# Top-k attention with a squared-ReLU feed-forward: the softmax sums by ScalarE's accumulator, their reciprocals by a power on GpSimd

## The chip, the cores and the metric

One core of a Trainium2 chip. The metric is the device time of one execution in microseconds; the median of the runs counts. The core's engines are named as in the profile: PE (TensorE; PEld are its weight loads), DVE (VectorE), ACT (ScalarE), POOL (GpSimd) and SP (SyncE, which here issues DMAs). Each works through its own queue in order.

## The reference

```python
B, H, S, D = q.shape                       # 8, 8, 576, 64
scores = np.matmul(q, k.transpose(0, 1, 3, 2)) / np.sqrt(D)
kth = np.partition(scores, -32, axis=-1)[..., -32:-31]
scores = np.where(scores >= kth, scores, -1e9)
scores = scores - np.max(scores, axis=-1, keepdims=True)
attn = np.exp(scores)
attn = attn / (np.sum(attn, axis=-1, keepdims=True) + 1e-09)
attn_out = np.matmul(attn, v)              # 8, 8, 576, 64
x = attn_out.transpose(0, 2, 1, 3).reshape(B * S, H * D)      # 4608 x 512
h = np.maximum(x @ w_in, 0.0)              # w_in 512 x 2048
out = (h * h @ w_out).astype(np.float32)   # w_out 2048 x 512
```

Of each row of 576 scores the 32 largest are kept, then softmax, then the product with the values; the result goes through two matrix products with a squared ReLU between.

## The kernel before

The attention is a list of 144 steps (`U = 144`). A step handles two row blocks of 128 rows (x = 0 and 1), mostly the same rows of two heads, so every tile of scores is 128 partitions x 2 x 576. The order of all instructions is written out by hand in one loop, `for u in range(U)`, and `pin` keeps each engine's queue in that order. Several steps are in work at once. In iteration u:

- GpSimd drops the entries of step u-1 that are under its 32nd largest: `drop` writes a very negative number, as bytes, into `gone` (L409, once per x), and a DMA issued by GpSimd adds that to the scores `s` (L413; in the first steps an addition on GpSimd, L411).
- VectorE runs the search for the 32 largest of step u: `quads_of` (L323, L324, which open an iteration on VectorE), then `topk` in four rounds of MAX8 (L374) and three of MATCH_REPLACE8 (L378). The last round is the pair of MAX8 over 576 columns (288 + 144 in the first 11 steps). Between rounds 2 and 3 stands `pairs_of(u+1)` (L314, L315).
- TensorE computes the scores of step u+1 (L285, two halves `sc_a`, `sc_b`); ScalarE copies them to `s` (L294). Between the two halves stands `in_gap`: the products of the weights with the values for step u-4 (`weigh`, L461), into the one accumulator `av`. The values carry a column of ones, so column 64 of the product is the sum of the weights.
- VectorE takes the reciprocal of that column (`invert`, L475), and ScalarE multiplies by it in `place` (L494, L499), both for step u-4.
- ScalarE computes the exponentials of step u-2 (`exps`, L417), and SP turns them by a transposing DMA into `wT` (`turn`, L426).
- GpSimd makes the smaller partners of pairs by integer arithmetic on the bits: `both(u+1)` (L338: sum of the two halves) and `lesser(u+1)` (L347: less the larger, which ScalarE's copy `most` (L330) gives it). The last round of MAX8 of step u+1 reads what L347 writes.
- In 40 of the steps GpSimd has one more small operation behind L347 on the results of `topk` (L384 to L386, 128 x 36).
- At the end come pieces of the feed-forward (`dense`, `piece`: L579, L586, L594, L630), two to three a step, and ScalarE's `negate` (L394: the negated largest and 32nd largest, for the exponentials and the drop).

So on GpSimd the order in an iteration is: two drops, DMA issue, `both`, `lesser`, now and then a test. On ScalarE it is: copies of scores, preparation of later heads, two placings, two exponentials, `most`, casts, `negate`, ReLU and square.

```python
if ok(u - 4):
    invert(u - 4)
...
if ok(u - 4):
    place(u - 4)
...
if ok(u - 2):
    exps(u - 2, 0)
    exps(u - 2, 1)
    turn(u - 2)
```

After the loop the products, reciprocals and placings of the last four steps follow; the last two steps use other PSUM banks and TensorE's transposes.

Of the kernel before, what the change touches and what calls it, by code (L numbers as in the profile page):

```python
# [13 lines left out]
f32 = mybir.dt.float32  # L14
# [9 lines left out]
def kernel(  # L24
# [9 lines left out]
    nc = tc.nc  # L34
# [10 lines left out]
    def pin(ins):  # L45
        tc.keep_in_program_order(ins)
        return ins
# [224 lines left out]
    def scores(u, between=None):  # L272
# [15 lines left out]
        if not between:  # L288
            half(js[1])
        s = scp.tile([128, 2, S], f32, name="s", bufs=4)  # L290
        st[u] = {"s": s, "ps": ps}
# [99 lines left out]
    def negate(u, ends):  # L391
        neg = small.tile([128, 2, 2], f32, name="neg", bufs=4)
# [22 lines left out]
    def exps(u, x):  # L415
        d = st[u]
        pin(nc.scalar.activation(w_two[u % 3][:, x, 0:S], d["s"][:, x, :], AF.Exp, bias=d["neg"][:, x, 0:1]))  # L417

# [5 lines left out]
    def turn(u):  # L424
        wT = scp.tile([128, 9, 128], bf16, name="wT", bufs=3)
        pin(nc.sync.dma_start_transpose(out=wT[:, :, :], in_=w_two[u % 3][:, :, :].rearrange("p x n -> p (x n)")))  # L426
        st[u]["wT"] = wT
# [7 lines left out]
    def turn_by_tensor(u, x):  # L435
        if "tp" not in st[u]:
            st[u]["wT"] = scp.tile([128, 9, 128], bf16, name="wT", bufs=3)
# [34 lines left out]

    def invert(u):
        r = small.tile([128, 2, 1], f32, name="rsum", bufs=4)
        pin(nc.vector.reciprocal(r[:, :, :], sums(u)[:, :, 64:65]))  # L475
        st[u]["r"] = r
# [206 lines left out]
    def most_ups(u):  # L683
        if u < U - 26:
            return 1 if downs else 2
        return 2 if u >= U - 20 or len(ups) > 4 else 1

    def in_gap(u):
        products(u - 4)
        if moves:  # L690
            moves.pop(0)()()
# [52 lines left out]
    pin(nc.gpsimd.memset(ones[:, :], 1.0))  # L744
    worst = const.tile([128, 1], f32, name="worst")
    load_weights(2)
    scores(0)
# [18 lines left out]
    def products(w):  # L766
        if ok(w):
            for x in range(2):
                weigh(w, x)
# [6 lines left out]
    for u in range(U):  # L776
# [18 lines left out]
        if u == 0:  # L795
            in_gap(u)
        if ok(u - 4):
            invert(u - 4)
        casts_next = bool(soon) and soon[0].__name__ == "values"
        for _ in range(0 if casts_next else 2 if u < 8 else 1):  # L800
            prepare(u)
        if ok(u - 4):
            place(u - 4)
        turn_x(u)
        moves.extend(soon_moves)
        soon_moves.clear()
        if u == U - 1:
            moves.pop(0)()()
            fill_scores(KH // 2)
        if ok(u - 2):  # L810
            exps(u - 2, 0)
            exps(u - 2, 1)
            turn(u - 2)
        fetch(4 if u < 12 else 3)
# [5 lines left out]
        if ok(u + 1):  # L820
            pairs_of(u + 1)
            copy_far(u + 1)
            lesser(u + 1)
            if tests:
                pin(tests.pop(0)())
        topk(u, (3,))
        if casts_next:
# [7 lines left out]
        if u < U - 1:  # L835
            dense(u, 0)
            st[u]["neg"] = negate(u, 2)
            dense(u, 1)
        else:
            piece(True)  # L840
            piece(True)
# [22 lines left out]
    one.square()  # L864
    invert(U - 4)
    place(U - 4)
# [11 lines left out]
    products(U - 3)  # L878
    invert(U - 3)
    place(U - 3)  # L880
# [152 lines left out]
```

## Time and profile before

| | |
|---|---|
| median of 3 runs | 905.09 us (904.73 to 907.03) |
| the profiled execution | 905.09 us |
| its span | 903.0 us |
| granted TensorE clock | 0.948 |
| busy: PE, DVE, ACT, POOL | 678.7, 881.8, 760.1, 779.0 us |

The profile shows one execution. A row of the timeline gives the start and the length in microseconds, the engine, the line of the kernel, the operation with what it writes and reads, how many in a row are merged (x2), and in brackets how long the engine had been idle before, with what ended that wait. A row of the groups gives the line, the operation, the count, busy time in us and mean length in ns, and then the idle time before these instructions and what ended it. Successive instructions of one engine overlap a little, so a length says less than the distance to the next start.

### The profile page before, as it was taken

How to read it: one execution, taken by the hardware profiler on the slowest of the kernel's cores; microseconds unless marked ns; L12 is line 12 of the kernel's file. 1: busy time of each engine (PE TensorE's matmuls, PEld its weight loads, DVE VectorE, ACT ScalarE, POOL GpSimd, SP SyncE). 2: the span in 40 equal slices, each digit the busy share in tenths (PEclk: the TensorE clock that was granted, in tenths of full speed). 3: DMA queues.
4: the chain of work that ended last, by engine and by line, in shares of the span. 5: the costliest groups of instructions: out<-in, count | busy, mean ns of one | idle time of the engine just before them, and what ended most of it. 6: DMA issues, size and time to landing. Idle time of an engine off the chain costs nothing.

```text
span 903.0 us, 21007 instructions
## 1 busy us (share of the span) xinstructions
PE 678.7 (75%) x6274; PEld 424.6 (47%) x6274; DVE 881.8 (98%) x3635; ACT 760.1 (84%) x1752; POOL 779.0 (86%) x818
## 2 busy tenths in 40 slices
PE   5777777777777777767687777677777777887796
PEld 3334454445444445444454444444444444554455
DVE  6999999999999999999999999999999999999995
ACT  3566799889988898888988899988999888997883
POOL 7999988988988888898898888998898988899880
PEclk9989999999999999999999999998999999999999
DMA  6699989899999999899899999999899999687762
GB/s 147 106 155 207 179 186 191 192 197 203 194 193 184 199 190 197 190 192 210 186 201 185 195 194 191 199 196 191 189 206 186 209 202 214 145 162 181 158 142 53
DMA packets 290778, 164.78 MB, mean 182 GB/s; under 512 B 258145, under 2 KB 268641, under 8 KB 290657
## 3 DMA queue, kind: packets, MB, share of 16 engines
q1 hardware_dynamic: 267408, 80.29, 48.0%
q0 software_dynamic: 21904, 82.65, 40.6%
q8 instruction: 52, 0.85, 0.4%
q14 instruction: 70, 0.57, 0.2%
q10 hardware_dynamic: 1344, 0.43, 0.2%
HBM read 37.75 MB, written 9.44 MB: 52 GB/s over the span
## 4 chain that ended last, share of the span: by engine, by line
DVE 74%; issue 12%; ACT 5%; PE 4%; DMA 2%; POOL 2%; SPq 0%; POOLq 0%; DVEq 0%; ACTq 0%
DVE m L374 31%; DVE cat L378 20%; DVE sc_b L314 6%; DVE most L315 5%; DVE cat L324 5%; DVE cat L323 5%; ACT s L294 1%; DVE rsum L475 1%; DMA s<-gone_b 1%; ACT rl L586 1%; DMA s<-gone_a 1%; POOL cat L347 1%; PE dn_ps L630 1%; PE sc_b L285 1%; ACT x_tok L494 0%
## 5 line engine op out<-in xcount | busy, mean ns | idle before, releaser
L374 DVE MAX8 m<-cat 128x8 f32<-128x104 f32 (+3 forms) x1152 | 435.4, 416 | 0.0
L378 DVE MATCH_REPLACE8 cat<-m,cat 128x104 f32<-128x104 f32 (+2 forms) x864 | 260.7, 306 | 0.0
L338 POOL TENSOR_TENSOR cat<-s 128x576 int32<-128x576 int32 (+1 forms) x144 | 238.6, 1657 | 2.7 <-ACT s L294 2.7
L347 POOL TENSOR_TENSOR cat<-cat,most 128x576 int32<-128x576 int32 (+1 forms) x144 | 196.1, 1362 | 25.0 <-DVE m L374 7.5
L285 PE MATMUL sc_b<-qkT 64*128 64x288 f32 x512 | 107.4, 494 | 88.4 <-DVE cat L324 84.2
L285 PE MATMUL sc_a<-qkT 64*128 64x288 f32 x512 | 97.3, 453 | 95.4 <-DVE most L315 39.2
L579 PEld LDWEIGHTS <-w_in 128*128 128x128 bf16 x2304 | 146.2, 101 | 38.6 <-issue 15.7
L630 PE MATMUL dn_ps<-w_out,h 128*128 128x512 bf16 x560 | 159.5, 416 | 0.3 <-ACT h L594 0.3
L579 PE MATMUL gen<-xT,w_in 128*128 128x128 bf16 x2016 | 137.1, 224 | 2.2 <-ACT xT L538 1.4
L409 POOL TENSOR_SCALAR gone_a<-s,neg 128x576 uint8<-128x576 f32 x143 | 107.1, 749 | 16.0 <-ACT neg L394 4.8
L409 POOL TENSOR_SCALAR gone_b<-s,neg 128x576 uint8<-128x576 f32 x142 | 106.3, 749 | 12.6 <-ACT neg L394 0.9
L294 ACT ACTIVATE s<-sc_b 128x576 f32<-128x576 f32 x144 | 93.4, 648 | 25.4 <-PE sc_b L285 21.5
L285 PEld LDWEIGHTS sc_a<-qkT 64*128 64x128 f32 x512 | 41.4, 186 | 123.4 <-issue 33.3
L294 ACT ACTIVATE s<-sc_a 128x576 f32<-128x576 f32 x144 | 91.3, 634 | 4.9 <-PE sc_a L285 3.2
L285 PEld LDWEIGHTS sc_b<-qkT 64*128 64x128 f32 x512 | 43.9, 198 | 103.8 <-PE av_ps L461 63.5
L394 ACT ACTIVATE neg<-m 128x4 f32<-128x4 f32 (+1 forms) x145 | 29.9, 206 | 70.6 <-DVE m L374 69.6
L594 ACT ACTIVATE h<-rl 128x512 bf16<-128x512 f32 x136 | 85.7, 630 | 4.3
L586 ACT ACTIVATE rl<-gen 128x512 f32<-128x512 f32 x142 | 83.0, 586 | 0.7 <-PE gen L579 0.6
L630 PEld LDWEIGHTS <-h 128*128 128x128 bf16 x560 | 53.3, 104 | 61.6 <-issue 26.3
L461 PEld LDWEIGHTS <-wT 128*128 128x128 bf16 (+1 forms) x1600 | 54.5, 100 | 54.4 <-issue 43.9
L413 POOL DMA_DIRECT2D s<-gone_b x67 | 59.3, 885 | 22.0 <-DVE m L374 9.0
L413 POOL DMA_DIRECT2D s<-gone_a x66 | 58.3, 884 | 20.4 <-DVE m L374 12.0
(172 smaller groups left out, 1248.6 us busy)
## 6 DMA issues: line engine op xcount, KB each, us to landing
s<-gone_b POOLq DMA_DIRECT2D x67, 576.0 KB, 4.6
s<-gone_a POOLq DMA_DIRECT2D x66, 576.0 KB, 4.8
v_raw<-in_v_dram SPq DMA_DIRECT2D x64, 128.0 KB, 3.3
k_raw<-in_k_dram SPq DMA_DIRECT2D x63, 128.0 KB, 3.4
q_raw<-in_q_dram SPq DMA_DIRECT2D x63, 128.0 KB, 3.2
out_dram<-wide SPq DMA_DIRECT2D x31, 256.0 KB, 3.0
v_raw<-in_v_dram SPq DMA_DIRECT2D x64, 32.0 KB, 3.0
w_in<-in_moe_w_in_dram POOLq DMA_DIRECT2D x8, 256.0 KB, 4.7
```

Of the source, the lines that this page charges most:

```text
L285: pin(nc.tensor.matmul(out=ps[j][:, x, 0:HALF], lhsT=lhsT, rhs=rhs, start=True, stop=True))
L294: pin(nc.scalar.activation(s[:, :, j * HALF:(j + 1) * HALF], ps[j][:, :, 0:HALF], AF.Copy))
L338: pin(tt(less, s[:, :, 0:wide].bitcast(i32), s[:, :, HALF:HALF + wide].bitcast(i32), op=ALU.add))
L347: pin(tt(less, less, d["most"][:, 0:n_h, :, :].bitcast(i32).rearrange("p h x n -> p x h n"), op=ALU.subtract))
L374: pin(nc.vector.max(out=m[r][:, x, :], in_=part(r, x)))
L378: pin(nc.vector.match_replace(out=part(r, x), in_to_replace=m[r][:, x, :], in_values=part(r, x), imm_value=NEG))
L409: pin(nc.gpsimd.tensor_scalar(byte[:, x, :, 1], s[:, x, :], scalar1=d["neg"][:, x, 1:2], scalar2=-HUGE, op0=ALU.add, op1=ALU.mult))
L413: pin(nc.gpsimd.dma_start(out=s[:, :, :].rearrange("p x n -> p (x n)"), in_=byte[:, :, :, :].rearrange("p x n two -> p (x n two)").bitcast ...
L579: pin(nc.tensor.matmul(out=hp[:, n * n_rows:(n + 1) * n_rows], lhsT=w_in[:, kh, (f0 + n) * 128:(f0 + n + 1) * 128], rhs=xt(kh), start=(kh ...
L586: pin(nc.scalar.activation(kept["rl"][:, :], hp, AF.Relu))
L594: pin(nc.scalar.activation(h2, flat, AF.Square))
L630: pin(nc.tensor.matmul(out=op[:, :], lhsT=held["h2"][:, f, c * 128:(c + 1) * 128], rhs=w_out[:, f, :], start=(f == 0), stop=(f == NF - 1)))
```

## The change

- The sum of the weights is no longer taken from the product: `exps` gives ScalarE's exponentials an accumulator output, `sums`, one column for each x, for all steps but the last two.
- The reciprocals of two steps (4 columns) are made together on GpSimd, as the sums to the power of -1; this stands behind `lesser(u+1)` and the test in every second iteration. VectorE keeps the reciprocals of the last two steps.
- The exponentials and the turning move from u-2 to u-3, the products and the placings from u-4 to u-5. From step `CATCH` = 121 on they catch up: iterations 121 and 122 hold three exponentials each, from 123 on they are at u-2 again; iteration 124 holds the products and placings of two steps, and from 125 on they are at u-4.
- Deeper buffers: `s` 5 for 4, `neg` 6 for 4, `wT` 4 for 3.

```diff
     def exps(u, x):
         d = st[u]
-        pin(nc.scalar.activation(w_two[u % 3][:, x, 0:S], d["s"][:, x, :], AF.Exp, bias=d["neg"][:, x, 0:1]))
+        if u % 2 == 0 and x == 0 and u < U - 2:
+            d["sums"] = small.tile([128, 2, 2], f32, name="sums", bufs=4)
+            st[u + 1]["sums"] = d["sums"]
+        total = d["sums"][:, u % 2, x:x + 1] if u < U - 2 else None
+        pin(nc.scalar.activation(w_two[u % 3][:, x, 0:S], d["s"][:, x, :], AF.Exp, bias=d["neg"][:, x, 0:1], accum_out=total))
...
     def invert(u):
+        if u < U - 2:
+            if u % 2 == 0:
+                both_r = small.tile([128, 2, 2, 1], f32, name="rboth", bufs=4)
+                pin(nc.gpsimd.tensor_tensor(both_r[:, :, :, 0], st[u]["sums"][:, :, :], minus[:, :, :], op=ALU.pow))
+                st[u]["r"], st[u + 1]["r"] = both_r[:, 0], both_r[:, 1]
+            return
         r = small.tile([128, 2, 1], f32, name="rsum", bufs=4)
         pin(nc.vector.reciprocal(r[:, :, :], sums(u)[:, :, 64:65]))
         st[u]["r"] = r
...
+    CATCH = 121
+
+    def to_weigh(u):
+        return u - 5 if u <= CATCH + 3 else u - 4
+
+    def to_raise(u):
+        if u < CATCH:
+            return [(u - 3, 0), (u - 3, 1)]
+        if u == CATCH:
+            return [(u - 3, 0), (u - 3, 1), (u - 2, 0)]
+        if u == CATCH + 1:
+            return [(u - 3, 1), (u - 2, 0), (u - 2, 1)]
+        return [(u - 2, 0), (u - 2, 1)]
+
     def in_gap(u):
-        products(u - 4)
+        products(to_weigh(u))
...
-        if ok(u - 4):
-            invert(u - 4)
...
-        if ok(u - 4):
-            place(u - 4)
+        if ok(to_weigh(u)):
+            place(to_weigh(u))
...
-        if ok(u - 2):
-            exps(u - 2, 0)
-            exps(u - 2, 1)
-            turn(u - 2)
+        for w, x in to_raise(u):
+            if ok(w):
+                exps(w, x)
+                if x == 1:
+                    turn(w)
...
             lesser(u + 1)
             if tests:
                 pin(tests.pop(0)())
+        for w, x in to_raise(u):
+            if ok(w) and x == 1 and w % 2:
+                invert(w - 1)
         topk(u, (3,))
...
             dense(u, 0)
             st[u]["neg"] = negate(u, 2)
             dense(u, 1)
+            if u == CATCH + 3:
+                products(u - 4)
+                place(u - 4)
```

`minus` is a constant tile of -1.0, set once. The two `invert` calls of steps `U - 4` and `U - 3` behind the loop are taken out.

More of the change, by code (lines that the diff above doesn't have):

```diff
@@ L289, in scores @@
             half(js[1])
-        s = scp.tile([128, 2, S], f32, name="s", bufs=4)
+        s = scp.tile([128, 2, S], f32, name="s", bufs=5)
         st[u] = {"s": s, "ps": ps}
@@ L391, in negate @@
     def negate(u, ends):
-        neg = small.tile([128, 2, 2], f32, name="neg", bufs=4)
+        neg = small.tile([128, 2, 2], f32, name="neg", bufs=6)
         got = st[u]["ends"] if ends == 2 else st[u]["ends"][:, :, 0:1]
@@ L424, in turn @@
     def turn(u):
-        wT = scp.tile([128, 9, 128], bf16, name="wT", bufs=3)
+        wT = scp.tile([128, 9, 128], bf16, name="wT", bufs=4)
         pin(nc.sync.dma_start_transpose(out=wT[:, :, :], in_=w_two[u % 3][:, :, :].rearrange("p x n -> p (x n)")))
@@ L436, in turn_by_tensor @@
         if "tp" not in st[u]:
-            st[u]["wT"] = scp.tile([128, 9, 128], bf16, name="wT", bufs=3)
+            st[u]["wT"] = scp.tile([128, 9, 128], bf16, name="wT", bufs=4)
             st[u]["tp"] = {}
@@ L745 @@
     worst = const.tile([128, 1], f32, name="worst")
+    minus = const.tile([128, 2, 2], f32, name="minus")
+    pin(nc.gpsimd.memset(minus[:, :, :], -1.0))
     load_weights(2)
@@ L864 @@
     one.square()
-    invert(U - 4)
     place(U - 4)
@@ L878 @@
     products(U - 3)
-    invert(U - 3)
     place(U - 3)
```

## The prediction

> **What bounds the kernel now.** I read the page's busy time and chain first, then the timeline of VectorE step by step, then GpSimd's and ScalarE's, because the change takes work from the first and gives it to the other two.
>
> ```profile
> PE 678.7 (75%) x6274; PEld 424.6 (47%) x6274; DVE 881.8 (98%) x3635; ACT 760.1 (84%) x1752; POOL 779.0 (86%) x818
> ...
> DVE 74%; issue 12%; ACT 5%; PE 4%; DMA 2%; POOL 2%; SPq 0%; POOLq 0%; DVEq 0%; ACTq 0%
> ```
>
> VectorE (DVE) is busy for 98% of the span and carries the chain. What a reciprocal is worth there can be read from the first steps, since none is issued before step 4. Timeline of VectorE, step 2 (none) and step 6 (one); columns are start, length, what:
>
> ```profile
> 23.28 0.44 DVE L323 TENSOR_TENSOR cat<-sc_b,most 128x288 f32<-128x288 f32 x1
> ...
> 29.58 0.44 DVE L323 TENSOR_TENSOR cat<-sc_b,most 128x288 f32<-128x288 f32 x1
> ...
> 48.60 0.44 DVE L323 TENSOR_TENSOR cat<-sc_b,most 128x288 f32<-128x288 f32 x1
> ...
> 50.13 0.16 DVE L475 RECIPROCAL rsum<-av_ps 128x2 f32<-128x2 f32 x1
> 50.20 0.45 DVE L374 MAX8 m<-cat 128x8 f32<-128x120 f32 x2
> ...
> 54.96 0.44 DVE L323 TENSOR_TENSOR cat<-sc_b,most 128x288 f32<-128x288 f32 x1
> ```
>
> L323 opens a step. Step 2 takes 29.58 - 23.28 = 6.30 us, step 6 takes 54.96 - 48.60 = 6.36: 0.06 more. The reciprocal shows 0.16 us, but the MAX8 behind it starts 0.07 after it, under its tail. So one costs the path about 0.065, not 0.16.
>
> From step 11 (drops by DMA, wider bit sums) the stretch to step 141 is steady:
>
> ```profile
> 75.74 0.79 POOL L347 TENSOR_TENSOR cat<-cat,most 128x288 int32<-128x288 int32 x1
> ...
> 79.56 1.41 DVE L374 MAX8 m<-cat 128x8 f32<-128x576 f32 x2
> 80.88 0.44 DVE L323 TENSOR_TENSOR cat<-sc_b,most 128x288 f32<-128x288 f32 x1
> ...
> 862.41 0.43 DVE L323 TENSOR_TENSOR cat<-sc_b,most 128x288 f32<-128x288 f32 x1
> ```
>
> That is 130 steps in 781.5 us, 6.01 each. GpSimd (POOL) serves the same step, and one step in full view shows how close it is:
>
> ```profile
> 399.29 1.41 POOL L347 TENSOR_TENSOR cat<-cat,most 128x576 int32<-128x576 int32 x1
> ...
> 403.95 1.40 DVE L374 MAX8 m<-cat 128x8 f32<-128x576 f32 x2
> 404.05 0.42 ACT L330 ACTIVATE most<-sc_b 128x288 f32<-128x288 f32 x1
> ...
> 405.07 1.40 POOL L347 TENSOR_TENSOR cat<-cat,most 128x576 int32<-128x576 int32 x1
> 405.27 0.43 DVE L323 TENSOR_TENSOR cat<-sc_b,most 128x288 f32<-128x288 f32 x1
> ...
> 406.57 1.57 POOL L409 TENSOR_SCALAR gone_a<-s,neg 128x576 uint8<-128x576 f32 x2
> ...
> 407.77 0.52 ACT L494 ACTIVATE x_tok<-av_ps,rsum 128x64 bf16<-128x64 f32 x2
> ...
> 408.17 1.46 ACT L417 ACTIVATE w_two_a<-s,neg 128x576 bf16<-128x576 f32 x2
> ...
> 409.05 1.73 POOL L338 TENSOR_TENSOR cat<-s 128x576 int32<-128x576 int32 x1
> ...
> 410.86 1.41 POOL L347 TENSOR_TENSOR cat<-cat,most 128x576 int32<-128x576 int32 x1
> ```
>
> From one L347 to the next there are 410.86 - 405.07 = 5.79 us: GpSimd's own cycle when nothing holds it up, though the page calls it 86% busy. Its lead is visible too: the L347 of 399.29 ends at 400.70, and the last MAX8 pair that reads it starts at 403.95, 3.25 later; at step 10 the same lead is 79.56 - 76.53 = 3.03.
>
> **The change, part by part.**
>
> *Reciprocals leave VectorE.* 140 of the 142 stand in the loop (steps 4 to 143), the other two in the tail. 140 x 0.065 = 9.1 us, if nothing else is late: steps of 5.94.
>
> *A power joins GpSimd*, 71 of them, 128 x 4, each behind L347 of every second step. It needs no wait of its own, because L347 already waits for the copy `most`, which ScalarE issues after the exponentials concerned. Behind it stand the next two drops, their DMA issue and both bit sums. No power is in the trace. The nearest rows are the small test operations at the same place, and the same ones in the tail:
>
> ```profile
> 464.74 1.41 POOL L347 TENSOR_TENSOR cat<-cat,most 128x576 int32<-128x576 int32 x1
> 466.10 0.31 POOL L384 TENSOR_TENSOR flags<-m 128x36 f32<-128x36 f32 x1
> 466.50 1.57 POOL L409 TENSOR_SCALAR gone_a<-s,neg 128x576 uint8<-128x576 f32 x2
> ...
> 470.77 1.42 POOL L347 TENSOR_TENSOR cat<-cat,most 128x576 int32<-128x576 int32 x1
> 472.14 0.27 POOL L385 TENSOR_TENSOR flags<-m 128x36 f32<-128x36 f32 x1
> 472.49 1.57 POOL L409 TENSOR_SCALAR gone_b<-s,neg 128x576 uint8<-128x576 f32 x2
> ...
> 879.83 2.38 POOL L384 TENSOR_TENSOR flags<-m 128x36 f32<-128x36 f32 x3 [2.17 <-DVE m L374]
> ```
>
> Without a test, L347 to the drop is 406.57 - 405.07 = 1.50; with L384 it is 1.76, with L385 1.72. So a plain small operation adds 0.26 or 0.22 to the cycle. L347 spends 1.41 on 576 elements, 0.0024 each, so four elements instead of 36 save 0.08: the low end is about 0.17. In the tail three L384 in a row take 0.79 each, or 0.65 net of the 0.14 by which a small operation overlaps its neighbours: the high end among small operations. A power is several arithmetic steps on each element, so it should lie above the plain ones; I take 0.45, the middle of 0.26 and 0.65. Nothing in the trace excludes more.
>
> The Trainium skill ("Perfetto Trace Analysis", GPSIMD Engine Instruction) says to time this engine by the spacing of starts, not by reported spans; the trace bears that out, since L384's 0.31 adds 0.26. By the span the low end would be 0.23 (0.31 less the same 0.08), and the sum below 4 us higher.
>
> GpSimd's reserve in those 130 steps follows from its cycle and these groups (busy, mean ns; idle before):
>
> ```profile
> L413 POOL DMA_DIRECT2D s<-gone_b x67 | 59.3, 885 | 22.0 <-DVE m L374 9.0 <-DVE cat L378 8.5 <-POOL gone_b L409 4.5
> L413 POOL DMA_DIRECT2D s<-gone_a x66 | 58.3, 884 | 20.4 <-DVE m L374 12.0 <-DVE cat L378 7.9 <-POOL gone_a L409 0.6
> L384 POOL TENSOR_TENSOR flags<-m 128x36 f32<-128x36 f32 x24 | 9.0, 379 | 2.2 <-DVE m L374 2.2
> L385 POOL TENSOR_TENSOR flags<-m 128x36 f32<-128x36 f32 x8 | 2.1, 266 | 0.0
> L386 POOL TENSOR_SCALAR flags<-flags 128x36 f32<-128x36 f32 x8 | 2.1, 263 | 0.1
> ```
>
> Seven of the eight groups of tests fall there: 21 x 0.26 + 14 x 0.22 = 8.5. The DMA issues idle 42.4 in all, 2.5 more than 133 x 0.30. So GpSimd needs 130 x 5.79 + 8.5 + 2.5 = 763.7 of 781.5 us: a reserve of 17.8. 67 powers there at 0.45 want 30.2, 12.4 too many. GpSimd then sets the step, at about 5.87 + 0.22 = 6.10, and the MAX8 pair waits for L347.
>
> *The lead cushions little.* The new chain behind L347 is power, two placings, two exponentials, `most`, and only then VectorE's next L323: 0.45 + 0.52 + 1.46 + 0.42, and 0.25 for the sums, is 3.1, while VectorE needs 405.27 - 403.95 = 1.32 from the MAX8 pair to L323. So a lead under 1.8 holds VectorE up through ScalarE, and 3.0 - 1.8 = 1.2 can be used. Four powers and seven shorter steps before step 11 take 4 x 0.45 + 0.45 = 2.25 of lead: 1.05 too many. They also save VectorE 7 x 0.065 = 0.45.
>
> The sum: 12.4 + 1.05 - 0.45 = 13.0 us. In general it is 71 x p - 19.0 for a power of p us, zero at 0.27, and not under -9.1 plus what the end costs.
>
> *Sums by ScalarE.* Two stretches of the middle and of the end (length; busy time of PE, PEld, DVE, ACT, POOL), and the placings:
>
> ```profile
> 261.21:381.27 120.06, 89.92 (x830) 56.69 (x831) 120.06 (x501) 105.98 (x245) 105.57 (x106) 0.93 0.93 190
> ...
> 760.04:820.41 60.37, 49.69 (x498) 32.70 (x499) 60.22 (x251) 56.35 (x127) 53.23 (x56) 0.97 0.78 162
> ...
> L494 ACT ACTIVATE x_tok<-av_ps,rsum 128x64 bf16<-128x64 f32 x252 | 65.8, 321 | 1.5 <-DVE rsum L475 1.5
> ```
>
> Each step gets two accumulator outputs, which the trace does not show: between nothing and 0.20 each, the spacing of two small operations (a pair of placings lasts 0.52, a single one 0.32). I take 0.12 each, 0.25 a step, the middle and a little. ScalarE (ACT) is idle 14.1 us in 20 steps of the middle, 0.70 a step, so 0.25, or even 0.40, hides. In steps 124 to 133 it is idle 0.40 a step: there 0.25 and the placings moved in step 124 (0.52) leave little, and I count 1.5 us if VectorE still sets the step, nothing if GpSimd does, since longer steps give more room.
>
> *One step further behind.* Exponentials wait for a sum by DMA issued two steps before instead of one; the transposes on SP keep their distance to the products, and the loads behind them stay in order. The catching up at 121 and 122 adds one exponential of 0.73 to each step, inside the same 0.70 or so of idle time and the lead. I count nothing; without that cover it is 1.5 us in all. Deeper buffers cost no time. The placings now wait for GpSimd, and with them queue exponentials, `most`, and on TensorE the next products, which need the accumulator free.
>
> **The rivals.**
>
> *The power is as cheap as a plain operation* (p under 0.23): for it, everything else of these four elements is overhead that L385 shows whole; against it, a power is not one addition. At 0.17 GpSimd needs 5.87 + 0.085 = 5.96 a step against VectorE's 5.94. The formula gives -6.9, VectorE's own floor is -9.1 + 1.5 = -7.6: about 898, faster. It decides below 0.23. The Trainium skill ("GPSIMD Engine Reference", 3.1 Elementwise) states about 2.6 cycles an element at 1.2 GHz for two inputs, by which four elements would be 9 ns and the operation nearly all dispatch; L347's 2.4 ns an element agrees for additions, and no run shows it for a power.
>
> *The power is several times dearer* (over 1.0): nothing speaks against it but that no such row exists. At 1.67, the net of GpSimd's longest arithmetic operation (L338, 410.86 - 409.05 = 1.81 to the next start, less 0.14), the formula gives +100: about 1005. GpSimd is the bound in any case.
>
> *It balances* (p of 0.23 to 0.31): within 2.7 us of 905.1, which is the 0.3% that a measurement of this kernel can tell from no change.
>
> *ScalarE becomes the bound:* it needs accumulators over 0.35 each, past the 0.20 that rows show; then steps are 5.30 + 0.70 and more, about 905 at 0.35 and 2.6 us more for each 0.01 beyond, inside the forecast's range.
>
> **How the numbers follow.** GpSimd-bound with p between 0.31 and 1.0: 0.53 (with ScalarE's case). Cheap power: 0.30. Balance: 0.07. Dear power: 0.10. So faster 0.30, same 0.07, slower 0.63. The profiled execution took 905.09 us (span 903.0 and 2.1 around it), which is the median of the runs, so no correction is needed: 905.1 + 13.0 = 918.1. The range runs from 897, where VectorE sets the step and the end costs little, to 955, which is p = 0.97; beyond it lie the dear powers and the rest of that tail.
>
> **What would show it.** Right: no reciprocals but the last two on VectorE; steps of about 6.10 from L323 to L323; VectorE idle before the 576-wide MAX8, released by GpSimd's L347; GpSimd's cycles alternating 5.79 and about 6.24; ScalarE's placings waiting for the power every second step; VectorE's busy time down while the span grows. Wrong: steps of 5.94 with VectorE never idle (cheap power); or VectorE waiting for ScalarE's copies with GpSimd early (ScalarE's case); or a power of over a microsecond.

## The result, and the profile after

| | before | changed |
|---|---|---|
| median of 6 runs | 904.9 us (903.78 to 907.03) | 996.46 us (982.67 to 1006.11) |
| ratio to before | | 1.0964 (1.0935 to 1.0994) |
| profiled execution, span | 905.09, 903.0 us | 1002.48, 1000.5 us |

The changed kernel is 91 us slower. The sign was forecast, the size was not: 918.1 was predicted, and 996 lies outside 897 to 955. The profiled execution is 6 us above the median; no reading below rests on a difference of that size. Medians are of all runs, while ratios and their 95% intervals, here and below, leave out the slow runs, those over 1.5% above the fastest of their kernel, of which the profiled execution of the changed kernel is one.

The page of the changed kernel, busy time and chain (L294 to L394 keep their lines; exponentials L421, transposing DMA L430, products L465, power L481, placings L504):

```profile
PE 709.1 (71%) x6201; PEld 443.8 (44%) x6278; DVE 880.4 (88%) x3493; ACT 783.8 (78%) x2036; POOL 850.7 (85%) x890
...
DVE 25%; DMA 24%; ACT 22%; POOL 11%; PE 10%; issue 7%; POOLq 0%; SPq 0%; DVEq 0%; ACTq 0%
DVE m L374 10%; DMA wT<-w_two_c 9%; DVE cat L378 7%; DMA wT<-w_two_a 6%; DMA wT<-w_two_b 5%; PE sc_b L285 4%; ACT w_two_b L421 4%; POOL cat L347 3%; ACT w_two_c L421 3%; POOL cat L338 3%; DMA s<-gone_b 3%; ACT w_two_a L421 3%; ACT x_tok L504 2%; POOL rboth L481 2%; ACT s L294 2%
```

VectorE's share of the chain fell from 74% to 25%, and DMA's rose from 2% to 24%: the transposing DMA that writes `wT`. GpSimd is busy 71.7 us more (850.7 against 779.0), 1.01 for each of the 71 powers, yet only 11% of the chain is GpSimd's.

Its groups, as before (busy, mean ns; idle before):

```profile
L374 DVE MAX8 m<-cat 128x8 f32<-128x104 f32 (+3 forms) x1152 | 439.7, 422 | 1.2 <-POOL cat L347 1.2
...
L314 DVE TENSOR_TENSOR sc_b<-sc_a,s 128x288 f32<-128x288 f32 x144 | 65.8, 457 | 59.5 <-ACT s L294 56.8 <-PE sc_a L285 2.6
...
L323 DVE TENSOR_TENSOR cat<-sc_b,most 128x288 f32<-128x288 f32 x144 | 64.3, 447 | 41.4 <-ACT most L330 39.9
...
L481 POOL TENSOR_TENSOR rboth<-sums,minus 128x4 f32<-128x4 f32 x71 | 73.5, 1035 | 1.1 <-ACT w_two_a L421 1.1
...
L421 ACT ACTIVATION_READ_ACCUMULATOR w_two_a<-s,neg 128x1 f32 x96 | 20.0, 209 | 0.0
```

The rows of VectorE before:

```profile
L314 DVE TENSOR_TENSOR sc_b<-sc_a,s 128x288 f32<-128x288 f32 x144 | 64.8, 450 | 2.6 <-PE sc_a L285 2.6
...
L323 DVE TENSOR_TENSOR cat<-sc_b,most 128x288 f32<-128x288 f32 x144 | 62.6, 435 | 0.3 <-ACT most L330 0.2
```

The power takes 1.035 us. VectorE waits 1.2 us for L347, where the prediction put the wait, and 56.8 + 39.9 us for ScalarE's copies. These are about the whole 97.5 us by which the span grew. The loss is not spread evenly: from step 11 to step 141 the median step is 5.95 us, shorter than the 6.00 before, but 26 of the 130 steps last over 7 us, and together they exceed that median by 92 us. And behind those copies, in the view of waits (total us, times, longest), first before, then changed:

```profile
ACT s L294 <- PE sc_b L285: 21.5, 38, 1.8
...
PEld L461 <- DMA wT<-w_two_b: 4.3, 6, 1.5
```

```profile
ACT s L294 <- PE sc_b L285: 79.8, 52, 9.2
...
PEld L465 <- DMA wT<-w_two_b: 56.6, 23, 7.1
...
PEld L465 <- DMA wT<-w_two_c: 43.3, 20, 8.1
...
ACT x_tok L504 <- POOL rboth L481: 14.9, 16, 2.0
```

The chain of a bad step can be read backwards: VectorE waits for the score copies, the copies for TensorE's scores, TensorE for the turned weights (the products stand between the two halves of the scores), and these for the DMA.

Two views of DMA issues (median us from issue to landing), first before, then changed:

```profile
s<-gone_b POOLq DMA_DIRECT2D x67, 576.0 KB, 4.6
...
wT<-w_two_b SPq DMA_TRANSPOSE x47, 4.5
```

```profile
s<-gone_b POOLq DMA_DIRECT2D x67, 576.0 KB, 5.4
...
wT<-w_two_b SPq DMA_TRANSPOSE x47, 6.0
```

The medians hide the worst: in the changed kernel 39 of 142 transposes land later than 8 us, in the kernel before none. Of the 22 issued 0.10 to 0.15 us behind GpSimd's accumulating DMA (L413), 21 are among the 39. They land after 10.4 us on average, the longest after 16.5. The other 18 late ones went out at other distances, 8 of them 0.05 to 0.5 us ahead of the accumulating DMA. The timeline of a step with a distance of 0.12 us shows why the two meet so exactly, GpSimd, ScalarE and SP merged by time:

```profile
250.25 1.41 POOL L347 TENSOR_TENSOR cat<-cat,most 128x576 int32<-128x576 int32 x1
...
256.04 1.40 POOL L347 TENSOR_TENSOR cat<-cat,most 128x576 int32<-128x576 int32 x1
257.41 0.30 POOL L384 TENSOR_TENSOR flags<-m 128x36 f32<-128x36 f32 x1
257.68 1.03 POOL L481 TENSOR_TENSOR rboth<-sums,minus 128x4 f32<-128x4 f32 x1
...
258.74 0.52 ACT L504 ACTIVATE x_tok<-av_ps,rboth 128x64 bf16<-128x64 f32 x2 [1.46 <-POOL rboth L481]
...
258.81 1.56 POOL L409 TENSOR_SCALAR gone_a<-s,neg 128x576 uint8<-128x576 f32 x2
...
259.15 0.77 ACT L421 ACTIVATE w_two_b<-s,neg 128x576 bf16<-128x576 f32 x1
259.82 0.20 ACT L421 ACTIVATION_READ_ACCUMULATOR w_two_b<-s,neg 128x1 f32 x1
259.91 0.77 ACT L421 ACTIVATE w_two_b<-s,neg 128x576 bf16<-128x576 f32 x1
260.57 0.19 ACT L421 ACTIVATION_READ_ACCUMULATOR w_two_b<-s,neg 128x1 f32 x1
...
260.67 0.93 POOL L413 DMA_DIRECT2D s<-gone_a  x1 [0.30 <-POOL gone_a L409]
...
260.79 1.35 SPq L430 DMA_TRANSPOSE wT<-w_two_b  x1
...
263.13 1.41 POOL L347 TENSOR_TENSOR cat<-cat,most 128x576 int32<-128x576 int32 x1
```

Once GpSimd is late, both branches start at the end of the same power: GpSimd's two drops and issue (1.9 us) and ScalarE's two placings and two exponentials (2.0 us). They are equally long by accident, so the two DMAs go out 0.12 us apart. This pair landed after 8.2 us. In a worse place, where the pair went out 0.12 us apart too and the transposing DMA landed after 16.5 us, the timeline of VectorE has this wait:

```profile
307.07 0.47 DVE L314 TENSOR_TENSOR sc_b<-sc_a,s 128x288 f32<-128x288 f32 x1 [7.79 <-ACT s L294]
```

### The profile page after: what moved, and what is told of

Same layout as the page of the kernel before. It is cut to its first block, busy times and chain, and to the rows that moved or that the text cites. A ratio compares the mean times of both kernels' runs of the same rounds, so it can differ in the third digit from the quotient of the medians.

```text
span 1000.5 us, 20900 instructions
## 1 busy us (share of the span) xinstructions
PE 709.1 (71%) x6201; PEld 443.8 (44%) x6278; DVE 880.4 (88%) x3493; ACT 783.8 (78%) x2036; POOL 850.7 (85%) x890
## 4 chain that ended last, share of the span: by engine, by line
DVE 25%; DMA 24%; ACT 22%; POOL 11%; PE 10%; issue 7%; POOLq 0%; SPq 0%; DVEq 0%; ACTq 0%
DVE m L374 10%; DMA wT<-w_two_c 9%; DVE cat L378 7%; DMA wT<-w_two_a 6%; DMA wT<-w_two_b 5%; PE sc_b L285 4%; ACT w_two_b L421 4%; POOL cat L347 3%; ACT w_two_c L421 3%; POOL cat L338 3%; DMA s<-gone_b 3%; ACT w_two_a L421 3%; ACT x_tok L504 2%; POOL rboth L481 2%; ACT s L294 2%
## 5 line engine op out<-in xcount | busy, mean ns | idle before, releaser
L347 POOL TENSOR_TENSOR cat<-cat,most 128x576 int32<-128x576 int32 (+1 forms) x144 | 195.8, 1360 | 39.9 <-ACT most L330 15.0
L589 PEld LDWEIGHTS <-w_in 128*128 128x128 bf16 x2304 | 151.7, 104 | 42.9 <-issue 23.1
L285 PE MATMUL sc_b<-qkT 64*128 64x288 f32 x512 | 115.0, 527 | 68.9 <-DVE cat L324 64.2
L640 PE MATMUL dn_ps<-w_out,h 128*128 128x512 bf16 x492 | 154.7, 439 | 9.8 <-issue 7.3
L294 ACT ACTIVATE s<-sc_b 128x576 f32<-128x576 f32 x144 | 93.2, 648 | 83.9 <-PE sc_b L285 79.8
L589 PE MATMUL gen<-xT,w_in 128*128 128x128 bf16 x2016 | 140.7, 227 | 2.6 <-ACT xT L548 1.1
L465 PEld LDWEIGHTS <-wT 128*128 128x128 bf16 (+1 forms) x1600 | 56.7, 104 | 168.6 <-DMA wT<-w_two_b 56.6
L314 DVE TENSOR_TENSOR sc_b<-sc_a,s 128x288 f32<-128x288 f32 x144 | 65.8, 457 | 59.5 <-ACT s L294 56.8
L323 DVE TENSOR_TENSOR cat<-sc_b,most 128x288 f32<-128x288 f32 x144 | 64.3, 447 | 41.4 <-ACT most L330 39.9
L294 ACT ACTIVATE s<-sc_a 128x576 f32<-128x576 f32 x144 | 91.2, 633 | 6.0 <-PE sc_a L285 4.3
L640 PEld LDWEIGHTS <-h 128*128 128x128 bf16 x560 | 56.3, 110 | 71.1 <-issue 39.7
L421 ACT ACTIVATE w_two_c<-s,neg 128x576 bf16<-128x576 f32 x94 | 72.5, 785 | 16.1 <-DMA s<-gone_b 15.7
```

The lines of the kernel that those rows point to most:

```text
L285: pin(nc.tensor.matmul(out=ps[j][:, x, 0:HALF], lhsT=lhsT, rhs=rhs, start=True, stop=True))
L294: pin(nc.scalar.activation(s[:, :, j * HALF:(j + 1) * HALF], ps[j][:, :, 0:HALF], AF.Copy))
L347: pin(tt(less, less, d["most"][:, 0:n_h, :, :].bitcast(i32).rearrange("p h x n -> p x h n"), op=ALU.subtract))
L589: pin(nc.tensor.matmul(out=hp[:, n * n_rows:(n + 1) * n_rows], lhsT=w_in[:, kh, (f0 + n) * 128:(f0 + n + 1) * 128], rhs=xt(kh), start=(kh ...
L640: pin(nc.tensor.matmul(out=op[:, :], lhsT=held["h2"][:, f, c * 128:(c + 1) * 128], rhs=w_out[:, f, :], start=(f == 0), stop=(f == NF - 1)))
```

## The experiments

The theories, as they developed. G: GpSimd's added load alone sets the time. C, later L: the late power ties ScalarE to GpSimd, the two DMAs collide, and the rest follows. S: the shift by a step costs something by itself. W: ScalarE's lateness counts, whether the DMAs meet or not. Every experiment has its own runs of the kernel before on the same chip, medians 904.7 to 907.5.

**Which part of the change costs.** e4 adds one unused power to the kernel before, in every second step, and nothing else of the change.

```diff
+        if ok(u - 3) and u % 2 == 0:
+            idle_r = small.tile([128, 2, 2], f32, name="idle_r", bufs=4)
+            pin(nc.gpsimd.tensor_tensor(idle_r[:, :, :], some[:, :, :], minus[:, :, :], op=ALU.pow))
```

> The kernel before, with nothing moved and no sums, and an unused power (128 x 4 of constants) on GpSimd at the place where the change has its powers, every second step. Theory C: the issues slip together as in the changed kernel, transposes land in 6 us or more on average, and it is over 960 us. Theory G: 71 x 0.97 - 18.5 over the kernel before, and nothing else: 950 to 958 us with VectorE waiting for GpSimd's bit sums at the wide MAX8. Theory S: no shift, so no collisions: as G, or less.

Measured: 992.7 us (988.01 to 997.9), ratio 1.0927 (1.0841 to 1.1013). The power alone is enough for a loss of this size, 35 us more than G had forecast. The way is not the one that C forecast either, as its waits show:

```profile
DVE cat L323 <- ACT most L330: 78.8, 43, 7.9
...
ACT w_two_c L417 <- DMA s<-gone_a: 49.0, 17, 8.2
...
ACT w_two_a L417 <- DMA s<-gone_a: 27.2, 16, 5.1
ACT w_two_b L417 <- DMA s<-gone_a: 26.5, 15, 8.3
```

In the old order the exponentials stand one step behind the accumulating DMA and wait for it directly when GpSimd is late; only 7 transposes land later than 8 us.

e1 keeps the change but multiplies where it raises to a power, so the normalisation is left out.

```diff
-  ... minus[:, :, :], op=ALU.pow))
+  ... minus[:, :, :], op=ALU.mult))
```

> The changed kernel with a multiplication in the place of the power (so the placings scale by minus the sum; the normalisation is left out), same place, same tiles. Theory C (collision): the power costs 0.97 us net every second step and so pushes GpSimd's next DMA issue (the drops' accumulating DMA) onto the moment at which SP issues the transposing DMA; the two then land in 9 us instead of 5, and products, scores and VectorE wait. With a multiplication at 0.17 to 0.25 net the two issues stay 0.8 us or more apart in nearly all steps: 895 to 903 us, DVE idle under 8 us, transposes landing in 4.8 us on average. Theory S (shift): running exponentials and transposes one step further behind, not the power, makes the DMAs collide, since the exponentials no longer wait for the accumulating DMA just issued: then it stays at 970 us or more. Theory G (GpSimd's load alone, by the prediction's formula 71 p - 19): 897 to 904, as C; C and G are told apart by e4 and e2.

Measured: 909.09 us (906.58 to 913.88), ratio 1.0035 (1.0006 to 1.0064). A cheap operation removes nearly the whole loss, so S falls. But it gains nothing either: the median step is 5.93 us, as worked out for VectorE without reciprocals, and about 10 us of waits for ScalarE's copies give it back:

```profile
DVE cat L323 <- ACT most L330: 6.6, 14, 1.0
...
DVE sc_b L314 <- ACT s L294: 3.4, 4, 1.4
```

Of these 10 us, 3.6 fall in steps 123 to 128, right behind the place where exponentials and placings catch up.

e3 makes the reciprocals of two steps together on VectorE, just ahead of the even placings; sums, shift and buffers stay.

```diff
-  pin(nc.gpsimd.tensor_tensor(both_r[:, :, :, 0], st[u]["sums"][:, :, :], minus[:, :, :], op=ALU.pow))
+  pin(nc.vector.reciprocal(both_r[:, :, :, 0], st[u]["sums"][:, :, :]))
```

> The changed kernel with the reciprocals of two steps (128 x 4) as one instruction on VectorE every second step, just ahead of the placings; ScalarE's sums, the shift by one step and the deeper buffers stay. Theories C and G: half of the reciprocals' 9.1 us is saved, ScalarE's two reads of the accumulator a step (0.09 to 0.2 us each) mostly hide: 898 to 905 us, DVE idle under 10 us. Theory S: 970 us or more.

Measured: 907.03 us (904.79 to 908.19), ratio 0.9989 (0.9957 to 1.002): the same as before. Its steps alternate between 5.93 us without a reciprocal and 6.00 with one, so half of the 9.1 us is saved; about as much goes to 4.9 us of VectorE's waits for ScalarE's copies, and 3.2 us of its idle time fall in steps 123 to 128 again.

e8 measures the price by itself: small operations in a row on GpSimd at the very end of the kernel before.

```diff
+    for n, op in ((4, ALU.mult), (1, ALU.pow), (4, ALU.pow), (16, ALU.pow)):
+        for z in range(3):
+            pin(nc.gpsimd.tensor_tensor(price[:, :], some[:, 0:n], minus[:, 0:n], op=op))
```

> The kernel before with twelve small operations on GpSimd in the tail, three each: a multiplication of 128 x 4, powers of 128 x 1, 128 x 4 and 128 x 16, on constants, results unused. The spacing of starts gives the price by itself. If the power's price is per element (about 0.2 us each on top of a plain operation): 0.4, 1.0 and 3.5 us. If it is mostly a fixed price: near 1 us for all three. The multiplication: 0.2 to 0.3.

Groups of that kernel (busy, mean ns of three):

```profile
L899 POOL TENSOR_TENSOR price_pow<-some,minus 128x16 f32<-128x16 f32 x3 | 8.6, 2896 | 0.0
...
L899 POOL TENSOR_TENSOR price_pow<-some,minus 128x4 f32<-128x4 f32 x3 | 3.5, 1176 | 0.0
...
L899 POOL TENSOR_TENSOR price_pow<-some,minus 128x1 f32<-128x1 f32 x3 | 1.9, 650 | 0.0
...
L899 POOL TENSOR_TENSOR price_mult<-some,minus 128x4 f32<-128x4 f32 x3 | 0.5, 203 | 0.0
```

By the distance of starts a power takes 0.52 to 0.57 us for one column, 0.98 for four and 2.87 for sixteen, so about 0.36 and 0.157 for each column (one of three was longer at one and at four columns, 0.80 and 1.48, which lifts those means and is left out here). A multiplication of four columns takes 0.15.

**How the late power does it.** e5 adds two unused powers to e3 at eight steps, 16.3 us in all, less than the reserve of 17.8.

```diff
+        if u % 16 == 0 and 16 <= u <= 128:
+            for _ in range(2):
+                pin(nc.gpsimd.tensor_tensor(idle_r[:, :, :], some[:, :, :], minus[:, :, :], op=ALU.pow))
```

> As e3 (no power in the work itself, 907 us), and at eight steps, 16 apart, two unused powers on GpSimd: 8 x 2.04 = 16.3 us of load in all, inside GpSimd's reserve of 17.8 us, and 2.04 at a time, inside its lead of 3 us. Theory C (a late GpSimd puts its accumulating DMA onto the transposing DMA, and the two slow each other down): each kick makes some transposes land in 8 us or more and costs 3 us or more of VectorE's time: 930 us and more. Theory G (GpSimd's load alone): nothing that VectorE sees, 905 to 910 us.

Measured: 922.2 us (917.13 to 932.03), ratio 1.0137 (1.0061 to 1.0213), between the two expectations. Behind six of the eight places VectorE waits 1.2 us or less in all before the next; behind the other two it has single waits of 4.1 and 6.4 us. Some 20 and 30 us after the powers of these two a pair had gone out 0.06 and 0.10 us apart, and its transposing DMA landed after 11.8 and 13.7 us.

e2 puts exponentials and turning of e3 ahead of the preparation and the placings, to bring the DMAs together without a power.

```diff
+        for w, x in to_raise(u):
+            if ok(w):
+                exps(w, x)
+                if x == 1:
+                    turn(w)
         for _ in range(0 if casts_next else 2 if u < 8 else 1):
             prepare(u)
         if ok(to_weigh(u)):
             place(to_weigh(u))
```

> As e3 (no power: the reciprocals of two steps in one on VectorE, from ScalarE's sums), and the exponentials and the transposing DMA stand ahead of the preparation and the placings in ScalarE's queue, so that the transpose goes out 0.5 to 1.1 us earlier, near the moment of GpSimd's accumulating DMA. No engine has more work than in e3. Theory C: transposes that go out within 0.3 us of an accumulating DMA land in 8 us or more, and the kernel is over 930 us, though GpSimd has no power at all. Theory G: no difference from e3 beyond 5 us. Theory S: as e3.

Measured: 905.93 us (904.25 to 919.94), ratio 1.0005 (0.9963 to 1.0047). A miss: only 10 of 142 transposes fell within 0.3 us of the other DMA, so it did not make the case that it was meant to test. Those ten landed after 4.6 to 6.9 us, not the 8 and more of theory C; two of them stood 0.10 to 0.15 behind. So such a distance does not make a transpose late every time.

e9 is the same order with the power. The placings that wait for it now stand behind the exponentials.

> The changed kernel, power and all, with the exponentials and the transposing DMA ahead of the preparation and the placings in ScalarE's queue (the order of e2, which cost nothing there). Theory L (lock): in the changed kernel the placings wait for the power, the exponentials stand behind them, and so the transposing DMA goes out at a fixed 0.12 us after GpSimd's accumulating DMA whenever GpSimd is late; those land in about 10 us and hold TensorE. Here the transposes no longer wait for the power: under 15 of 142 land later than 8 us (39 in the changed kernel), and what remains is GpSimd's load: 945 to 965 us. If a late GpSimd does the harm by itself, lock or not: 980 us or more.

Measured: 967.09 us (962.42 to 973.35), ratio 1.0685 (1.0635 to 1.0734), 29 us less than the changed kernel with the same work, and 2 us over the expectation. No transpose lands later than 8 us. VectorE's waits:

```profile
DVE cat L323 <- ACT most L330: 33.8, 65, 2.6
DVE m L374 <- POOL cat L347: 17.8, 58, 1.2
...
DVE sc_b L314 <- ACT s L294: 3.8, 4, 2.1
```

The wait for the score copies has gone from 56.8 to 3.8 us, and the predicted wait for L347 is there. GpSimd's cycles are 5.79 and 6.82 us and the median step 6.31. This order does two things at once, though: it parts the two DMAs, and it takes the exponentials out of the chain from the power to the copy `most`.

e12 is e9 with a multiplication, the control for the order; the normalisation is left out.

> As e9 with a multiplication in the place of the power (the normalisation is left out), 0.15 us by e8: what the change could have brought at best with a free power. The prediction's rival of a cheap power: 898 us. Going by e1 (909 us), where VectorE lost 9 us to ScalarE's copies although its step was 5.93: 900 to 908 us, the less the more of that came from placings that wait.

Measured: 923.71 us (910.43 to 939.06), ratio 1.0108 (1.0041 to 1.0175). A miss: with GpSimd on time, this order brings 21 transposes within 0.2 us of the other DMA, and 16 land later than 8 us. The collision needs no power. (The four runs lie between 910 and 939 us, and the late transposes are those of the one that took 927.)

e6 and e7 put the exponentials further ahead still, before the score copies; e6 with the power, e7 with e3's reciprocals.

> The changed kernel, power and all, with the exponentials and the transposing DMA ahead of ScalarE's copies of the next scores, some 2.3 us earlier. GpSimd's load is the same. Theory C: the transposes now go out before the accumulating DMA, and a GpSimd that falls behind moves away from them instead of onto them; what is left is GpSimd's load: 71 x 1.02 - 19 = 53 over the kernel before, 950 to 965 us, with VectorE waiting for L347's result at the wide MAX8 and few transposes over 8 us. If transposes and accumulating DMAs don't matter to each other: 985 us or more, as the changed kernel.

> The control of e6: as e3 (reciprocals of two steps on VectorE), with the exponentials and the transposing DMA ahead of the copies of scores. What the new order costs by itself: the copies of scores are 1.6 us later, of 1.0 to 1.4 us that they have to spare, so 905 to 930 us by either theory; transposes that go out within 0.3 us of the accumulating DMA should land in 7 us or more by C, in 5 us if the distance doesn't matter.

Measured: e6 985.14 us (980.31 to 985.39), ratio 1.0843 (1.0779 to 1.0906); e7, its control, 971.02 us (961.07 to 986.62), ratio 1.0692 (1.0618 to 1.0766). Inconclusive: the order alone delays the score copies, for which VectorE waits 45.3 us in e7, and costs some 65 us. e6 has 2 late transposes and e7 19, and yet e6 took the 985 us that were forecast for the case that the two DMAs do not matter to each other.

e10 puts the preparation of later heads between placings and exponentials of the changed kernel.

> The changed kernel, power and all, with the preparation of later heads (0.2 to 0.7 us of ScalarE in about three steps of four) between the placings and the exponentials instead of ahead of the placings. Theory L: the fixed distance of 0.12 us grows to 0.3 to 0.8 us in the steps that have such a piece, at which transposes land in 6 to 7 us: 950 to 980 us, clearly under the changed kernel's 996. If the lock doesn't matter: 990 us or more.

Measured: 997.96 us (984.37 to 1001.29), ratio 1.0936 (1.0857 to 1.1015). A miss: this is the time that was forecast for the case that the lock does not matter, but the order did not part the pairs. Many steps have no such piece, 15 pairs still go out 0.10 to 0.14 apart, and 27 transposes land later than 8 us.

e11 raises one column only, at half the price and near the 0.45 of the prediction; three of four reciprocals are left out.

```diff
-  ... both_r[:, :, :, 0], st[u]["sums"][:, :, :], minus[:, :, :], op=ALU.pow))
+  ... both_r[:, 0, 0, :], st[u]["sums"][:, 0, 0:1], minus[:, 0, 0:1], op=ALU.pow))
```

> The changed kernel with a power of one column (128 x 1) for each pair of steps, which all four placings then use (three of four reciprocals are left out). By the prices in e8 the power is then 0.52 us by itself, about the 0.45 of the prediction. The prediction's formula, 71 p - 19: +16 to +18, so 920 to 925 us. Theory L: GpSimd is over its reserve all the same, so its lead runs out and some transposes are locked to the accumulating DMA: 925 to 950 us.

Measured: 950.95 us (946.0 to 964.95), ratio 1.0484 (1.0442 to 1.0525). At 0.52 the prediction's formula gives 905.1 + 17.9 = 923, so a right price alone would still have been 28 us short. 25 transposes land later than 8 us, 16 of all went out 0.10 to 0.15 behind.

**Moving the pair apart, and the pair by itself.** e13 and e14 only add work to the changed kernel: one unused ScalarE copy (`range(1)`) and two (`range(2)`) in the branch behind the power.

```diff
         if ok(to_weigh(u)):
             place(to_weigh(u))
+        if u % 2 and 5 <= u < CATCH:
+            for z in range(1):
+                pin(nc.scalar.activation(spare_out[:, :], spare[:, :], AF.Copy))
```

> The changed kernel, power and all, with one unused ScalarE copy (128x64) between the placings and the exponentials of every odd iteration up to 119, the iterations whose placings wait for a power: 58 pieces of added work, about 0.26 us each by the distance of two placings. Theory L (two equal branches): from the start of a power, the accumulating DMA is issued 2.99 us later (power, two drops, issue) and the transposing DMA 3.11 us later (power, two placings, two exponentials), so whenever GpSimd is late and the placings wait, the two go out 0.12 apart and both crawl. The added copy makes it about 0.38. Then under 12 transposes land later than 8 us (39 in the changed kernel) and the kernel gets faster by the added work: 950 to 975. Rival W (the loss is lateness of ScalarE behind the power, coincidence or not): 58 x 0.26 = 15 us more, 1000 to 1015.

> The same with two unused copies, so that the two DMAs go out about 0.64 apart. Theory L: as with one copy or up to 10 us slower, 950 to 985, again with few slow transposes. Rival W: 30 us over the changed kernel, 1015 to 1030.

Measured: e13 990.47 us (986.21 to 1001.45), ratio 1.0929 (1.0834 to 1.1024); e14 982.19 us (978.52 to 988.55), ratio 1.0795 (1.071 to 1.0881). In both the cluster moved as intended (51 transposes at 0.15 to 0.30 us, 57 at 0.45 to 0.60), and 12 instead of 39 land later than 8 us. With two copies the kernel is faster than the changed one without them, the intervals of the ratios being apart; with one they overlap. Rival W, which had 1015 to 1030 for e14, falls in this form; that ScalarE's lateness costs something too is not excluded. L's size for e13 was missed by 15 us: the copies stand in the chain from the power to VectorE, and that wait is now the large one in e14:

```profile
DVE cat L323 <- ACT most L330: 64.9, 67, 6.7
DVE sc_b L314 <- ACT s L294: 9.4, 7, 3.3
...
ACT x_tok L504 <- POOL rboth L481: 34.8, 37, 1.6
```

e15 is their control: the one copy added to e3.

> The control: the reciprocals of two steps on VectorE instead of the power (907.03 without the copy), with the one unused ScalarE copy of every odd iteration. Both theories: ScalarE has some 0.5 us idle a step, so 905 to 915. If it is over 920, ScalarE has no such room and the other two runs cannot be read as bare shifts.

Measured: 906.58 us (903.97 to 908.35), ratio 0.9981 (0.9951 to 1.0012). ScalarE hides the copies while GpSimd is on time.

e18 adds e14's two copies to e11.

> The changed kernel with the power of one column only (three of four reciprocals left out), which without more took 950.95, and two unused ScalarE copies between the placings and the exponentials of odd iterations. The formula of the prediction at this power's own 0.52 us gives 905.1 + 71 x 0.52 - 19.0 = 923. Theory L: with the two DMAs moved apart the kernel gets faster than 951 in spite of the copies, 925 to 942, with under 8 transposes over 8 us (25 without the copies). Rival W (ScalarE's lateness alone): 951 to 980.

Measured: 944.04 us (937.57 to 951.74), ratio 1.0433 (1.0362 to 1.0504), 2 us over L's range; 6 late transposes instead of 25. Against e11 the intervals overlap, so the 7 us are not proved. The counts are of profiled executions, e11's at 964.95 us its longest and e18's at 937.57 its shortest, so they may overstate the difference.

e16 and e17 run the pair of DMAs alone, at the end of the kernel before; a VectorE fill of n columns sets the distance.

```diff
+    for n in (0, 150, 210, 260, 300, 340, 380, 420, 480) * 3:
+        pin(nc.vector.memset(turned_two[:, 0, 0:1], 0.0))
+        pin(nc.vector.memset(s_two[:, 0, 0:1], 0.0))
+        pin(nc.gpsimd.dma_start(out=s_two[...], in_=gone[0][...], accum_op=ALU.add))
+        if n:
+            pin(nc.vector.memset(wait_two[:, 0:n], 0.0))
+        pin(nc.vector.memset(w_two[0][:, 0, 0:1], 0.0))
+        pin(nc.sync.dma_start_transpose(out=turned_two[:, :, :], in_=w_two[0][...]))
```

> The kernel before, with the disputed pair of DMAs by itself at the end: 20 times, one after the other, an accumulating DMA from GpSimd and a transposing DMA from SP of the loop's sizes, started by VectorE one right behind the other, one 576-wide fill apart, four fills apart, and each alone, four of each. Nothing else moves then. If the pair alone is enough, those started within 0.15 us land in about 10 us and the others in 4 to 6. If the rest of the loop's traffic is needed, all of them land in 4 to 6. The time is longer by about 20 x 7 us and means nothing else.

> The kernel before, with the pair of DMAs by itself at its end once more, 27 times one after the other, the transposing DMA started from 0.28 us before to 0.25 us behind the accumulating one in nine steps of a VectorE fill (150 to 480 columns), three of each. The pair 0.28 before and 0.33 behind landed in 4.4 and 5.6 us alone on the queues (alone 3.2, the accumulating one 4.1). Theory P (two DMAs that start together take turns packet by packet, whatever else moves): those between 0 and 0.14 land in about 8 to 10 us. Rival T (it takes the rest of the loop's traffic): all stay under 6.5.

e16 (1012.55 us, with the added work) missed the distance in question: its pairs stood 0.22 to 0.28 before, 0.33 and 2.5 behind, and the transposing DMA landed after 4.4 to 6.9, 5.5 and 3.3 us; alone after 3.2, the accumulating one alone after 4.1. e17 (1096.93 us) hit it. Three of its pairs in the timeline; the next fill of VectorE waits for the landing:

```profile
919.80 0.86 POOL L911 DMA_DIRECT2D s_two<-gone_a  x1 [7.33 <-DVE w_two_a L914]
919.86 1.27 SPq L915 DMA_TRANSPOSE turned_two<-w_two_a  x1
...
930.98 0.06 DVE L909 MEMSET turned_two<- 128x1 bf16 x1 [11.16 <-DMA turned_two<-w_two_a]
...
931.43 0.86 POOL L911 DMA_DIRECT2D s_two<-gone_a  x1 [10.76 <-DVE s_two L910]
931.53 1.30 SPq L915 DMA_TRANSPOSE turned_two<-w_two_a  x1
...
938.62 0.06 DVE L909 MEMSET turned_two<- 128x1 bf16 x1 [7.14 <-DMA turned_two<-w_two_a]
...
945.68 0.86 POOL L911 DMA_DIRECT2D s_two<-gone_a  x1 [5.75 <-DVE s_two L910]
...
945.86 1.48 SPq L915 DMA_TRANSPOSE turned_two<-w_two_a  x1
...
951.72 0.06 DVE L909 MEMSET turned_two<- 128x1 bf16 x1 [5.90 <-DMA turned_two<-w_two_a]
```

The issue to landing times of the transposing DMA, 27 pairs in all: 4.3 to 7.1 us from 0.53 to 0.22 before (the 7.1 was the first pair of all), 5.4 to 5.8 at 0.11 before, 6.1 to 7.6 at 0.04 before, 10.6 to 11.0 at 0.06 behind, 6.9 to 7.5 at 0.10, 5.8 to 5.9 at 0.14, 5.5 to 5.9 from 0.18 on. The pair is slow by itself, with a sharp peak, so T falls; P's 8 to 10 us hold only near 0.06, and at 0.14 the pair stays under T's 6.5. At the 0.12 of the changed kernel's pairs, which land after 10.4 us in the loop, the pair by itself therefore takes some 6 to 7 (an estimate between the rows at 0.10 and 0.14): there the loop adds something that this run does not have. In the loop most of the late transposes stand from 0 to 0.15 behind.

## Why the prediction was right in sign and wrong in size

**Right.** The reciprocal's 0.065 on VectorE: where GpSimd is on time, e1's median step is 5.93 us against the 5.94 worked out. GpSimd's own cycle: 5.79 from L347 to L347 (250.25 to 256.04), and 6.82 with a power (7.09 to 263.13, where the test L384 adds 0.27). The accumulator outputs: each is an instruction of its own, 0.209 long, and the next start comes 0.09 later than without it (in the step shown, at 259.91 instead of 259.82); 0.12 was taken. Whether it hides wholly is not shown: e1 and e3, on time on GpSimd, have 10 and 4.9 us of waits for ScalarE's copies, against 0.2 before, and part of these belong to the catching up. The placings do wait for the power. That GpSimd becomes the limit is borne out by e9.

**Wrong: the price of the power.** The step "it should lie above the plain ones; I take 0.45, the middle of 0.26 and 0.65" failed. The cycles with a power are 1.03 longer; by itself it takes 0.98. It scales with the columns, while the rows it was bounded by are nearly all overhead. This size was left to the dear-power rival, with 0.10. The formula itself held roughly: 71 x 1.03 - 19.0 = 54.1, or 959, and e9, where the DMAs keep apart, took 967. The 41.2 us that the wrong price left out, 71 x (1.03 - 0.45), are the larger part of the error of 78.

**Wrong: what a late GpSimd does.** "One step further behind ... I count nothing", on the ground that the transposes keep their distance, was the second failure. In the order of the program they keep their distance to the products, but not in time to the accumulating DMA on GpSimd's queue, which the step did not look at. The prediction even named the wait that ties ScalarE to GpSimd, and summed the branch of placings and exponentials; it did not sum GpSimd's branch from the same power and see that the two are equal. Of the 37 us that remain between 959 and 996, 29 go away when the exponentials stand ahead of the waiting placings (e9), which also shortens the chain to `most`, and 14 in spite of added work when the branch is merely lengthened (e14). So about 14 are shown to go with the meeting of the DMAs; how the rest divides between it and ScalarE's wait for the power is not shown. e11 shows that the loss beyond the formula comes near the predicted price too: 28 us above it.

**Wrong: the signature.** VectorE idle before MAX8 for L347 was foretold and is 1.2 us; ScalarE's copies hold it instead. Steps of about 6.10 throughout were foretold, or 6.4 at the true price (5.87 + 67 x 1.03 / 130); the median is 5.95, and the loss sits in the 26 long steps. The foretold wait appears (17.8 us) in e9, with a median step of 6.31.

**The cheap-power rival was wrong as well.** At 0.15 us (e1) it forecast about 898; e1 took 909. VectorE's 9.1 us were saved and lost again to waits for ScalarE's copies, which the sum had hidden in ScalarE's average idle time of 0.70 a step. For the catching up and the steps behind it, it had allowed 1.5 us or nothing; steps 123 to 128 alone cost 3.6 in e1 and 3.2 in e3. So the change has no gain to give at any price of the power that was tried, and e3 and e2 only equal the kernel before.

**Open.** Why two DMAs that start within 0.1 us of each other crawl is not shown, only that they do. In e7 many pairs 0.1 to 0.2 apart landed in 6 to 7 us, so the loop's traffic matters to the exact place of the peak. In the changed kernel 8 of the 9 pairs in which the transposing DMA went out 0.05 to 0.5 ahead were late too, which the pair by itself does not show. The granted TensorE clock fell from 0.948 to 0.894 with the longer waits; whether that added to them was not separated. The 8 us between e9 and the formula, and the 21 between e18 and it, are not assigned.

## What to carry to other kernels

When work is added to an engine that is close to its limit, follow from that instruction every branch to its next DMA issue and compare the lengths: if they are equally long, a common late start puts the two DMAs on the queues together each time. Price an operation that has no row by measuring it alone at two widths before it goes into a sum; neighbours of another kind bound the overhead, not the arithmetic. An average of idle time on the engine that is to hide the added work is no cover for the steps in which it has none.

## What the runs showed of the hardware

- A power on GpSimd takes 0.36 us and 0.157 for each column of 128 partitions (e8, 1, 4 and 16 columns); a multiplication of four columns 0.15.
- An accumulator output on ScalarE is a second instruction, 0.209 us long, of which 0.09 count.
- A transposing DMA (128 x 1152, 16 bit) issued 0.06 us behind an accumulating DMA (576 KB) takes 10.8 us where it takes 3.2 alone, 5.8 from 0.14 and 5.7 from 0.18 on (e17, e16); both are slowed alike (10.7 against 4.1 for the accumulating one).
